# Chunk 0's first channel product as seven block products, its sums on GpSimd

## The chip, the cores and the metric

The kernel runs on one core of a Trainium2 chip. The metric is the device time of one execution in microseconds (us). In the rows below the engines are PE (TensorE, matrix products), PEld (its loading of weights), DVE (VectorE), ACT (ScalarE), POOL (GpSimd) and SP (SyncE, which here only issues transfers). Each engine runs its own instructions strictly in program order and waits on semaphores for the others.

## The reference

Three layers follow one another on 2 batches of 768 tokens, 512 wide:

```
x = attention(q, k, v)          # window of 16 keys to either side, and 24 block summaries
u = x + (relu(x^T @ w_tok1) @ w_tok2)^T            # mixes tokens
y = u + relu(u @ w_ch1) @ w_ch2                    # channel product, width 1536 inside
k = relu((mu_k*y + (1-mu_k)*y_prev) @ w_k)         # second expert layer
r = sigmoid((mu_r*y + (1-mu_r)*y_prev) @ w_r)
out = r * ((k*k) @ w_v)
```

The change concerns `u @ w_ch1`, for the first third of the tokens.

## The kernel before, in words

The 1536 tokens (both batches in a row) are cut into three chunks of 512, numbered 0 to 2. Chunk 0 lies in batch 0 alone, and is ready while the attention of batch 1 still runs, so its channel product shares the engines with that attention. The inner width of 1536 is cut into three blocks d of 512.

Every float32 operand of a large product is held as a high and a low part in a rounded format, and a product takes three matmuls, high by high, high by low and low by high (`mm3`, lines 190 to 192). The high part of a tensor is made on ACT, the low part on DVE by a subtraction. Weights come from memory in packed form, and `ca`, `cn` (ACT) and `cj` (DVE, line 410) unpack them, before `ch` (ACT) and `cl` (DVE, line 417) split them.

The first channel product is computed in two ways:

- Chunk 0: directly. `ch1` (PLAN op `c1`) makes one of 12 tiles of 128 by 512 by 4 by 3 matmuls of 512 columns, from `uc` (u, kept split) and the split weights `wc`. `c1h` and `c1l` (line 469) apply relu and split the result.
- Chunks 1 and 2: by a scheme in which a product of 2 by 2 blocks takes seven block products instead of eight (`product`, op `p`). For each d, each of the seven takes 4 by 3 matmuls of 256 columns. `x_sum` (`bs`, line 643) makes four sums and differences of blocks of u, `x_high` and `x_low` (`bh`, `bl`, line 656) split the seven forms of u. The seven forms of the weights need `form_sum` (`ws e`, line 443), `form_high` (`wh e`) and `form_low` (`wl e`, line 451). `prod_copy` (`pc`, ACT) and seven `prod_add` (`pa`, line 708, DVE) put the seven results together in `ev`, and `h2_high`, `h2_low` (`gh`, `gl`, line 582) apply relu and split.

In the kernel before, the weights of the block products ("e") of d = 0 and 1 are loaded and unpacked a second time (`rawe`); three of the seven forms of d = 1 and 2 are the split weights that chunk 0 uses (`HELD`). Forms are stored to DRAM (`wst`) and loaded again (`wld`) for chunk 2.

The order of all work is written out by hand in the string `PLAN`: the order of its ops is the order of the instructions on each engine. All transfers go through SP's one queue in that order (`load`, line 195), and gates (ops that begin with `g`, such as `gu` and `gx`) are transfers of one element that hold back this queue until the tile they read is there. POOL copies overlapping pieces of v (`vu`, lines 246 to 249) and sets small edges (`pad`, line 317, and `ye`).

Of the kernel before, what the change touches and what calls it, by code (L numbers as in the profile page):

```python
# [55 lines left out]
gv 10,vu 10,gv 11,vu 11,km 1 0,vs 1 10,t2 0 2 0,ca c 0 0,t2l 0 1 0,km 1 3,cj c 0 0,ld c 1 0,t2 0 3 0,ch c 0 0,ca c 1 0
cj c 1 0,gu 0 1 0,t2h 0 2 0,t2l 0 2 0,ch c 1 0,vs 1 11,vs 1 12,sc 6,t2h 0 3 0,cl c 0 0,sc 8,vd 1,t2l 0 3 0,t2 0 0 1,lq 1 2
pad 6,cl c 1 0,t2 0 1 1,max 6,en 6,pad 7,t2h 0 0 1,sc 7,t2h 0 1 1,ef 6,max 7,tr 6 0,pad 8,sc 9,tr 6 1,tc 6 0,max 8,tc 6 1
en 7,t2 0 2 1,pad 9,t2h 0 2 1,ef 7,sc 10,max 9,tr 7 0,en 8,tc 7 0,tr 7 1,pv 6,pad 10,max 10,tc 7 1,ef 8,en 9,ef 9,tr 8 0
norm 6,tr 8 1,sc 11,tc 8 0,tc 8 1,en 10,tr 9 0,pad 11,max 11,ef 10,tr 9 1,pv 7,tc 9 0,tc 9 1,xh 6,t2 0 3 1,en 11,xl 6,ef 11  # L60
norm 7,c1 0 0,t2h 0 3 1,xh 7,xl 7,tr 10 0,c1h 0 0,pv 8,tc 10 0,c1l 0 0,tr 10 1,c1 0 1,norm 8,xh 8,xl 8,tc 10 1,tr 11 0
c1h 0 1,pv 9,tc 11 0,c1l 0 1,tr 11 1,pv 10,norm 9,tc 11 1,xh 9,pv 11,t1 6,xl 9,t1 7,norm 10,xh 10,norm 11,gq 1 0,gq 1 2
ld c 0 1,ca c 0 1,xl 10,gq 1 1,ld c 2 0,ld c 3 0,gu 0 3 1,ld c 1 1,ld c 2 1,ld c 3 1,ca c 3 0,gx 10,ld c 5 1,t1 8,gx 8
ld c 4 0,ld c 5 0,cn c 0 1,ld c 7 0,ca c 2 0,cj c 0 1,cn c 2 0,ld c 4 1,gx 9,ld c 6 0,ld c 6 1,ch c 0 1,cl c 0 1,ld c 11 0
t1 9,cn c 3 0,ld c 8 0,cj c 2 0,ca c 1 1,cj c 3 0,c2 0 0 0,ch c 2 0,c2 0 0 1,ld c 10 0,ch c 3 0,cl c 2 0,cn c 1 1,c2 0 0 2
cl c 3 0,ca c 2 1,ld c 9 0,c2 0 0 3,cj c 1 1,cn c 2 1,c1 0 2,ch c 1 1,cj c 2 1,cl c 1 1,ch c 2 1,ld c 8 1,ca c 5 0,cl c 2 1
t1 10,ca c 4 0,cn c 4 0,c1h 0 2,cj c 4 0,cn c 5 0,c2 0 1 0,c1l 0 2,c2 0 1 1,cj c 5 0,ca c 3 1,ch c 4 0,cl c 4 0,c2 0 1 2
# [101 lines left out]
def block_kernel(ctx: ExitStack, tc: tile.TileContext, qT, kT, vp, w1, w2, wc, wk, wv, wr, mu, mask, const, out):  # L169
# [386 lines left out]
    def ch1_low(c, f):  # L556
        relu_low(h2[c, f], h2p.pop((c, f)))
# [348 lines left out]
```

## Time and profile before

| | |
|---|---|
| median of 3 runs | 457.58 us (457.46 to 459.58) |
| the profiled execution | 462.69 us, of which the span from first to last instruction is 460.9 us |
| mean granted TensorE clock in it | 0.995 |
| PE, DVE, ACT, POOL busy | 447.9, 362.7, 278.4, 39.9 us |

The profiled execution has 1.8 us outside of its span. Busy times are read with care: instructions of one engine overlap somewhat, so the distance between two starts in a row, and not the duration of one, is what an instruction costs an engine that is full.

### The profile page before, as it was taken

How to read it: one execution, taken by the hardware profiler on the slowest of the kernel's cores; microseconds unless marked ns; L12 is line 12 of the kernel's file. 1: busy time of each engine (PE TensorE's matmuls, PEld its weight loads, DVE VectorE, ACT ScalarE, POOL GpSimd, SP SyncE). 2: the span in 40 equal slices, each digit the busy share in tenths (PEclk: the TensorE clock that was granted, in tenths of full speed). 3: DMA queues.
4: the chain of work that ended last, by engine and by line, in shares of the span. 5: the costliest groups of instructions: out<-in, count | busy, mean ns of one | idle time of the engine just before them, and what ended most of it. 6: DMA issues, size and time to landing. Idle time of an engine off the chain costs nothing.

```text
span 460.9 us, 10730 instructions
## 1 busy us (share of the span) xinstructions
PE 447.9 (97%) x4316; PEld 392.0 (85%) x4316; DVE 362.7 (79%) x576; ACT 278.4 (60%) x504; POOL 39.9 (9%) x110
## 2 busy tenths in 40 slices
PE   8799999999999999999999999999999999999996
PEld 3567877888888878989898988888989999999995
DVE  3558978477678637989968819998899989999865
ACT  1377447489987443386635437996887773854530
POOL 1660880000000000000000000000000000000000
PEclk9989999999999999999999999999999999999999
DMA  7767641659745500680597795792979994984902
GB/s 253 233 198 239 202 134 46 233 171 399 300 155 173 219 0 1 221 327 2 173 401 295 279 392 240 297 392 112 352 255 372 369 402 141 348 301 155 337 7 91
DMA packets 33347, 106.23 MB, mean 230 GB/s; under 512 B 3730, under 2 KB 7314, under 8 KB 33298
## 3 DMA queue, kind: packets, MB, share of 16 engines
q1 hardware_dynamic: 33298, 105.55, 62.5%
q8 instruction: 34, 0.56, 0.5%
q14 instruction: 15, 0.12, 0.1%
HBM read 78.79 MB, written 26.74 MB: 229 GB/s over the span
## 4 chain that ended last, share of the span: by engine, by line
PE 83%; DMA 7%; POOL 4%; SPq 3%; DVE 1%; issue 1%; ACT 0%; DVEq 0%; POOLq 0%
PE p L190 9%; PE p L191 9%; PE p L192 9%; PE acc L191 7%; PE acc L192 7%; PE acc L190 7%; PE v L192 4%; PE v L191 4%; PE v L190 4%; DMA rawt<-in_w 3%; SPq L195 3%; PE r L190 2%; PE r L192 2%; PE h L191 2%; PE r L191 2%; PE h L192 2%
## 5 line engine op out<-in xcount | busy, mean ns | idle before, releaser
L708 DVE TENSOR_TENSOR ev<-p,ev 128x512 f32<-128x512 f32 x84 | 56.5, 688 | 19.5 <-PE p L192 16.9
L190 PE MATMUL p<-xs,wba 128*128 128x256 f32 x168 | 47.4, 282 | 0.0
L192 PE MATMUL v<-wbv,k 128*128 128x256 f32 x168 | 47.1, 281 | 0.0
L192 PE MATMUL p<-xs,wba 128*128 128x256 f32 x168 | 47.1, 281 | 0.0
L191 PE MATMUL p<-xs,wba 128*128 128x256 f32 x168 | 47.1, 280 | 0.0
L190 PE MATMUL v<-wbv,k 128*128 128x256 f32 x168 | 47.1, 280 | 0.0
L191 PE MATMUL v<-wbv,k 128*128 128x256 f32 x168 | 47.1, 280 | 0.0
L190 PE MATMUL acc<-hq,wc 128*128 128x512 f32 x96 | 37.8, 393 | 0.0
L191 PE MATMUL acc<-hq,wc 128*128 128x512 f32 x96 | 37.8, 393 | 0.0
L192 PE MATMUL acc<-hq,wc 128*128 128x512 f32 x96 | 37.7, 393 | 0.0
L578 ACT ACTIVATE hq<-ev 128x512 fp32r<-128x512 f32 x24 | 14.9, 631 | 34.3 <-DVE ev L708 31.6
L190 PEld LDWEIGHTS p<-xs,wba 128*128 128x128 f32 x168 | 31.7, 189 | 0.3
L191 PEld LDWEIGHTS p<-xs,wba 128*128 128x128 f32 x168 | 31.7, 189 | 0.1
L190 PEld LDWEIGHTS v<-wbv,k 128*128 128x128 f32 x168 | 31.7, 189 | 0.0
L192 PEld LDWEIGHTS v<-wbv,k 128*128 128x128 f32 x168 | 31.7, 189 | 0.0
L191 PEld LDWEIGHTS v<-wbv,k 128*128 128x128 f32 x168 | 31.7, 189 | 0.0
L192 PEld LDWEIGHTS p<-xs,wba 128*128 128x128 f32 x168 | 31.7, 189 | 0.0
L190 PE MATMUL p<-xs,wae 128*128 128x256 f32 x88 | 24.9, 283 | 0.9 <-DVE ev L708 0.9
L191 PE MATMUL p<-xs,wae 128*128 128x256 f32 x88 | 24.8, 282 | 0.0
L192 PE MATMUL p<-xs,wae 128*128 128x256 f32 x88 | 24.7, 280 | 0.0
L701 ACT COPY ev<-p 128x512 f32<-128x512 f32 x12 | 7.1, 590 | 26.4 <-PE p L192 26.4
L712 ACT ACTIVATE ev<-ev 128x512 f32<-128x512 f32 x24 | 15.0, 631 | 12.4 <-DVE ev L708 12.2
(171 smaller groups left out, 1316.8 us busy)
## 6 DMA issues: line engine op xcount, KB each, us to landing
wba<-kepta SPq DMA_DIRECT2D x28, 512.0 KB
wbv<-keptv SPq DMA_DIRECT2D x28, 512.0 KB
rawc<-in_wc SPq DMA_DIRECT2D x24, 512.0 KB
kepta<-waa SPq DMA_DIRECT2D x14, 512.0 KB
wbe<-kepte SPq DMA_DIRECT2D x14, 512.0 KB
keptv<-wav SPq DMA_DIRECT2D x14, 512.0 KB
rawe<-in_wc SPq DMA_DIRECT2D x8, 512.0 KB
kepte<-wae SPq DMA_DIRECT2D x8, 512.0 KB
```

Source lines behind the costliest of these rows:

```text
L190: PE.matmul(o, lhsT=wh, rhs=xh, start=start, stop=False)
L191: PE.matmul(o, lhsT=wh, rhs=xl, start=False, stop=False)
L192: PE.matmul(o, lhsT=wl, rhs=xh, start=False, stop=stop)
L195: nc.sync.dma_start(out=out, in_=in_)
L578: A.activation(out=h2_block(c, d, q, 0), in_=x, func=AF.Relu)
L701: A.copy(out=block(z, c, d, 0), in_=pr[z, c, d, 0])
L708: V.tensor_tensor(out=block(z, c, d, o), in0=pr[z, c, d, p], in1=block(z, c, d, x), op=ALU.add)
L712: A.activation(out=x, in_=x, func=AF.Relu)
```

## The change

Chunk 0's first channel product is computed by the seven block products too. `ch1` and the split copy `uc` are gone: u of chunk 0 is written unsplit into `y`, as in the other chunks. The block differences of all chunks (`bs` of the channel product) and the weight sums (`ws e`) move from DVE to POOL. All seven forms of the weights of every d are made before chunk 0 needs them, from the one raw load, stored to DRAM, and loaded again for chunks 1 and 2 (`WHICH`). The op counts in `PLAN` change like this: `c1`, `c1h`, `c1l` 12 to 0 each; `p` of the channel product 42 to 63; `pa` 84 to 105 in all; `pc` 12 to 15; `gh`, `gl` 24 to 36; `bh`, `bl` 14 to 21; `bs` 8 to 12; `wh e`, `wl e` 15 to 21; `ws e` 12 as before; `t2l`, `yl` 4 to 0; `ld e` with its `ca`, `cn`, `cj` 8 to 0; `ch c`, `cl c` 24 to 12; `cn c` 22 to 20; `wst e` 14 to 21; `wld e` 14 to 28. The whole string `PLAN` is written anew; chunk 0's and d = 1's block products stand where `c1` stood, and the products of the other chunks take the order d = 2, 1, 0 for chunk 1 and 0, 1, 2 for chunk 2, as before. The number of instructions goes from 563 to 549 on DVE, from 2571 to 2680 on PE, from 110 to 135 on POOL (as the compiled program lists them).

```diff
-norm 7,c1 0 0,t2h 0 3 1,xh 7,xl 7,tr 10 0,c1h 0 0,pv 8,tc 10 0,c1l 0 0,tr 10 1,c1 0 1,norm 8,xh 8,xl 8,tc 10 1,tr 11 0
...
-    HELD = {0: 0, 1: 1, 3: 3}
-
     def form_raw(z, d, j, w):
-        key = ("c", 4 * d + j, 0) if z == "e" and d == 2 else (z, d, j)
-        return words(cv[key], F32)[w]
...
+        return words(cv[("c", 4 * d + j, 0) if z == "e" else (z, d, j)], F32)[w]
...
-        V.tensor_tensor(out=form_raw(z, d, dst, 1), in0=form_raw(z, d, *x), in1=form_raw(z, d, *y),
+        (G if z == "e" else V).tensor_tensor(out=form_raw(z, d, dst, 1), in0=form_raw(z, d, *x), in1=form_raw(z, d, *y),
                         op=ALU.add if z != "v" and j == 0 else ALU.subtract)
...
-    def form_load(z, d, p, n=None):
-        key = (z, d, p) if n is None else (z, d, p, n)
+    def form_load(z, d, p, n):
+        key = (z, d, p, n)
...
+        if (c, dt // 2) not in ys:
+            ys[c, dt // 2] = slot([P, 2, CH + 1], f"y{c}_{dt // 2}")
+        return yk(c, dt)[:, 1 + off:1 + off + n], ps
...
-        A.copy(out=dst if W2[b][g][0] else dst[:, 0], in_=ps)
-
-    def tok2_low(*a):
-        dst, ps = upart(*a)
-        V.tensor_tensor(out=dst[:, 1], in0=ps, in1=dst[:, 0], op=ALU.subtract)
...
+        A.copy(out=dst, in_=ps)
...
-        h = (h2[c, f][:, 0, :], h2[c, f][:, 1, :]) if c == 0 else [hq[c, f // 4, f % 4 // 2, i][:, f % 2, :] for i in range(2)]
+        h = [hq[c, f // 4, f % 4 // 2, i][:, f % 2, :] for i in range(2)]
...
-        V.tensor_tensor(out=xsum(z, c, j), in0=x, in1=y, op=ALU.subtract)
+        (V if z else G).tensor_tensor(out=xsum(z, c, j), in0=x, in1=y, op=ALU.subtract)
...
+    WHICH = {(0, 0): (), (0, 1): (), (0, 2): (), (1, 2): (), (1, 1): (1,), (1, 0): (1,), (2, 0): (1,), (2, 1): (2,), (2, 2): (2,)}
+
     def product(z, c, d, p):
-        if z:
+        if z or c == 0:
             pr[z, c, d, p] = psum(f"p{z}{c}_{d}_{p}")
...
-        w, x = wa["a", d, p, TURN[c, d]] if z else form("e", d, p), xs[z, c, p]
+        w, x = wa["a", d, p, TURN[c, d]] if z else wa[("e", d, p) + WHICH[c, d]], xs[z, c, p]
```

On POOL, around the scores of batch 1, the program before has only the last edges of the attention tiles `e` and then nothing until the edges of `y`, whose tiles are the result of the channel product:

```order
L317 MEMSET e_1392 128x8x8
L317 MEMSET e_1459 128x8x8
L596 MEMSET y_0_2426 128x2
L596 MEMSET y_1_2428 128x2
L598 COPY y_1_1302<-y_1_2428 128x2
L598 COPY y_0_1195<-y_0_2426 128x2
```

After the change the block differences (`xt`, from the blocks of `y`) and the weight sums (in place in `rawc`) stand there, one edge of an attention tile (`e_1408`, query tile 9) behind the first of them, and an instruction named ISA ahead of all:

```order
L320 MEMSET e_1251 128x8x8
L320 MEMSET e_1320 128x8x8
L565 MEMSET y_0_1006 128x2
L608 ISA
L608 TENSOR_TENSOR xt_0_1406<-y_0_1006 128x512
L320 MEMSET e_1408 128x8x8
L437 TENSOR_TENSOR rawc_0_1018<-rawc_0_1018,rawc_0_1067 128x512
L565 MEMSET y_1_1086 128x2
L608 TENSOR_TENSOR xt_0_1406<-y_1_1086,xt_0_1406 128x512
L437 TENSOR_TENSOR rawc_0_994<-rawc_0_1018,rawc_0_994 128x512
L608 TENSOR_TENSOR xt_1_1543<-y_1_1086,y_0_1006 128x512
L608 TENSOR_TENSOR xt_1_1543<-y_1_1086,xt_0_1406 128x512
```

Four sums for d = 1 and four for d = 2 follow directly, then the eight differences of chunks 1 and 2. So POOL gets 24 subtractions and additions, and the tile 9 edge moved behind one of them.

On DVE, at the place of chunk 0's third and fourth direct tiles, the program before unpacks and splits weights (`rawc`, `wc`) and splits the relu of a direct tile (`h`):

```order
L417 TENSOR_TENSOR wc_0_1911<-rawc_0_1797,wc_0_1911 128x512
L410 SCALAR_TENSOR_TENSOR rawc_1_1782<-rawc_1_1782 128x512
L377 TENSOR_TENSOR xhl_1934<-xf_2_1757,xhl_1934 128x512
L417 TENSOR_TENSOR wc_1_1939<-rawc_1_1782,wc_1_1939 128x512
L410 SCALAR_TENSOR_TENSOR rawc_1_1805<-rawc_1_1805 128x512
L469 SCALAR_TENSOR_TENSOR h_0_3_1948<-h_0_3_1915,h_0_3_1948 128x512
L417 TENSOR_TENSOR wc_1_1956<-rawc_1_1805,wc_1_1956 128x512
```

After it, the additions of the block products (`ev`), the low parts of the forms of the weights of d = 1 (`wae`), the unpacking and the splits of the sums (`hq`) stand there without a break:

```order
L412 SCALAR_TENSOR_TENSOR rawc_1_1845<-rawc_1_1845 128x512
L445 TENSOR_TENSOR wae_0_1969<-rawc_0_1814,wae_0_1969 128x512
L552 SCALAR_TENSOR_TENSOR hq_011_1999<-ev_0_1_1723,hq_010_1973 128x2x256
L675 TENSOR_TENSOR ev_0_0_1560<-p_0_3_1945,ev_0_0_1560 128x512
L552 SCALAR_TENSOR_TENSOR hq_001_1820<-ev_0_0_1560,hq_000_1812 128x2x256
L445 TENSOR_TENSOR wae_1_1979<-rawc_0_1818,wae_1_1979 128x512
L552 SCALAR_TENSOR_TENSOR hq_011_1999<-ev_0_0_1560,hq_010_1973 128x2x256
L445 TENSOR_TENSOR wae_5_2032<-rawc_0_1814,wae_5_2032 128x512
L445 TENSOR_TENSOR wae_6_2038<-rawc_0_1848,wae_6_2038 128x512
L445 TENSOR_TENSOR wae_3_1982<-rawc_0_1848,wae_3_1982 128x512
L675 TENSOR_TENSOR ev_1_1_2050<-p_1_1_2013,ev_1_0_2029 128x512
```

Most of these have both inputs in SBUF (the `ev` rows and the `h` row read one from PSUM). So the making of the forms and the putting together of the products moved from a place behind chunk 0 into it.

## Rows read from the trace of the kernel before

**Rows 1.** The page, part 1 and part 2 (busy tenths in 40 slices)

```profile
PE 447.9 (97%) x4316; PEld 392.0 (85%) x4316; DVE 362.7 (79%) x576; ACT 278.4 (60%) x504; POOL 39.9 (9%) x110
POOL 1660880000000000000000000000000000000000
```

**Rows 2.** Waits of PE: line, awaited engine and tile: total us, times, longest

```profile
PE p L190 <- DVE ev L708: 0.9, 1, 0.9
...
PE u L499 <- DVE uc L538: 0.7, 2, 0.5
```

**Rows 3.** Windows: start:end length, busy us of each engine, clock, DMA share, GB/s

```profile
80.00:100.00 20.00, 20.00 (x421) 16.20 (x418) 11.26 (x21) 11.55 (x23) 0.00 (x0) 1.00 0.56 187
100.00:120.00 20.00, 20.00 (x88) 16.21 (x87) 14.39 (x23) 18.52 (x34) 0.00 (x0) 1.00 1.00 383
120.00:140.00 20.00, 20.00 (x96) 16.47 (x96) 15.74 (x26) 17.64 (x33) 0.00 (x0) 1.00 0.48 179
...
180.00:200.00 20.00, 19.12 (x148) 18.26 (x147) 18.82 (x32) 9.85 (x18) 0.59 (x1) 1.00 0.57 205
```

**Rows 4.** Timeline of PE: a direct tile's first matmul, and what follows its twelve

```profile
81.83 0.39 PE L190 MATMUL h<-uc,wc 128*128 128x512 f32 x1
...
84.62 0.60 PE L339 MATMUL et<-cst,e 128*128 128x128 f32 x4
```

**Rows 5.** Timeline of PE: 24 matmuls of block products (first, and next after them)

```profile
175.86 0.28 PE L190 MATMUL p<-xs,wc 128*128 128x256 f32 x1
...
178.65 0.28 PE L190 MATMUL p<-xs,wae 128*128 128x256 f32 x1
```

**Rows 6.** Groups of DVE instructions: busy us, mean ns, idle before them

```profile
L708 DVE TENSOR_TENSOR ev<-p,ev 128x512 f32<-128x512 f32 x84 | 56.5, 688 | 19.5 <-PE p L192 16.9
...
L443 DVE TENSOR_TENSOR rawe<-rawe,rawe 128x512 f32<-128x512 f32 x8 | 5.3, 688 | 0.1
```

**Rows 7.** Timeline of DVE, two instructions back to back

```profile
121.07 0.68 DVE L410 SCALAR_TENSOR_TENSOR rawc<-rawc 128x512 uint32<-128x512 uint32 x1
121.67 0.68 DVE L417 TENSOR_TENSOR wc<-rawc,wc 128x512 fp32r<-128x512 f32 x1
```

**Rows 8.** Timeline of DVE, 46 to 53 us

```profile
47.20 0.88 DVE L377 TENSOR_TENSOR xhl<-xf,xhl 128x512 fp32r<-128x512 f32 x1
48.00 1.69 DVE L410 SCALAR_TENSOR_TENSOR rawt<-rawt 128x512 uint32<-128x512 uint32 x2
49.62 1.09 DVE L417 TENSOR_TENSOR wt<-rawt,wt 128x512 fp32r<-128x512 f32 x1
50.98 0.69 DVE L469 SCALAR_TENSOR_TENSOR h<-t,h 128x512 fp32r<-128x512 f32 x1 [0.26 <-ACT h L466]
51.58 0.94 DVE L417 TENSOR_TENSOR wt<-rawt,wt 128x512 fp32r<-128x512 f32 x1
```

**Rows 9.** Timeline of POOL, 46 to 53 us

```profile
46.73 0.80 POOL L246 COPY vw<-vw 32x520 f32<-32x520 f32 x1 [15.15 <-DMA vw<-in_vp]
...
49.19 0.99 POOL L246 COPY vw<-vw 32x520 f32<-32x520 f32 x1
...
51.36 0.61 POOL L246 COPY vw<-vw 32x520 f32<-32x520 f32 x1
```

**Rows 10.** Timeline of POOL, its last before 164 us

```profile
67.18 0.57 POOL L317 MEMSET e<- 128x64 f32 x6
```

**Rows 11.** Timeline of PE: transposes of tile 9, then a product with v, then u

```profile
78.61 0.87 PE L339 MATMUL et<-cst,e 128*128 128x128 f32 x6
79.41 0.72 PE L350 MATMUL xo<-vbd,et 64*128 64x130 f32 x8
...
80.85 0.44 PE L499 MATMUL u<-cst,xf 128*128 128x128 f32 x2
```

**Rows 12.** DMA issues: the second loads of weights, KB each

```profile
rawe<-in_wc SPq DMA_DIRECT2D x8, 512.0 KB
```

More of the change, by code (lines that the diff above doesn't have):

```diff
@@ new lines @@
+bs 1 1 0,bs 1 1 1,bh 1 1 1,pa 1 0 1 6,v 0 0 6,fs 0 1 3,rst 2 0,bh 1 1 5,bs 1 1 2,fr 0 1 1,bl 1 1 1,vc 0 0,wld v 1 5 0
+fs 0 1 2,ks 0 1 0,fs 0 1 1,bh 1 1 4,bh 1 1 6,bl 1 1 5,v 0 0 1,bh 1 1 2,bl 1 1 6,v 0 0 2,ks 0 1 1,fh 0 1 4,wld v 1 6 0
+bl 1 1 2,fh 0 1 5,fl 0 1 5,v 0 0 3,bs 1 1 3,wld v 1 4 0,bh 1 1 3,ks 0 1 2,p 1 1 1 0,wld v 1 0 0,bl 1 1 4,fh 0 1 1,bl 1 1 3
+wld v 1 1 0,fh 0 1 6,fl 0 1 4,p 1 1 1 1,pc 1 1 1,fl 0 1 6,fh 0 1 3,wld v 1 2 0,ks 0 1 3,p 1 1 1 5,pa 1 1 1 0,fr 1 1 0
+fh 0 1 2,wld v 1 3 0,fl 0 1 1,fs 1 1 0,pa 1 1 1 1,p 1 1 1 6,pa 1 1 1 2,wld a 0 0 1,fh 1 1 0,fl 0 1 3,p 1 1 1 4,mp 2 0 0
@@ L382, in block_kernel @@
                "c": lambda f, i: wc[f][:, 512 * i:512 * i + 512], "r": lambda i: wr[i], "v": lambda d, j: wv[:, d, j],
[L383 to L384 removed]
+               "a": lambda d, j: wk[:, d, j]}
     def fetch(*key):
@@ L420, in block_kernel @@
     wa, kept = {}, {}
-    HELD = {0: 0, 1: 1, 3: 3}
     def form_raw(z, d, j, w):
-        key = ("c", 4 * d + j, 0) if z == "e" and d == 2 else (z, d, j)
-        return words(cv[key], F32)[w]
-    def form(z, d, p):
-        if (z, d, p) not in wa and z == "e" and d and p in HELD:
-            return wt["c", 4 * d + HELD[p], 0]
-        return wa[z, d, p]
+        return words(cv[("c", 4 * d + j, 0) if z == "e" else (z, d, j)], F32)[w]
     FORMS = {"A": (((0, 0), (1, 0), (1, 1), (3, 0), (2, 1), (0, 1), (3, 1)),
@@ L454, in form_store @@
         kept[z, d, p] = d_p.tile([P, 2, 512], F32, tag=f"{z}{d}{p}", name=f"kept{z}{d}_{p}")
-        load(kept[z, d, p], form(z, d, p).bitcast(F32))
-    def form_load(z, d, p, n=None):
-        key = (z, d, p) if n is None else (z, d, p, n)
+        load(kept[z, d, p], wa[z, d, p].bitcast(F32))
+    def form_load(z, d, p, n):
+        key = (z, d, p, n)
         wa[key] = slot([P, 2, 512], f"wb{z}{d}_{p}", F32R)
         load(wa[key].bitcast(F32), kept[z, d, p])
-    h1, uc, t1, ups = {}, {}, {}, {}
+    h1, t1, ups = {}, {}, {}
     def relu_high(dst, ps):
@@ L519, in upart @@
         ps = ups[b, dt, g][:, 0:n]
-        if c:
-            if (c, dt // 2) not in ys:
-                ys[c, dt // 2] = slot([P, 2, CH + 1], f"y{c}_{dt // 2}")
-            return yk(c, dt)[:, 1 + off:1 + off + n], ps
-        if (c, dt) not in uc:
-            uc[c, dt] = slot([P, 2, CH], f"uc{c}_{dt}", F32R)
-        return uc[c, dt][:, :, off:off + n], ps
+        if (c, dt // 2) not in ys:
+            ys[c, dt // 2] = slot([P, 2, CH + 1], f"y{c}_{dt // 2}")
+        return yk(c, dt)[:, 1 + off:1 + off + n], ps
     def tok2_gate(b, dt, g):
-        dst = upart(b, dt, g)[0]
-        gate(dst[:, 0:1] if W2[b][g][0] else dst[:, 1, 0:1].bitcast(F32))
+        gate(upart(b, dt, g)[0][:, 0:1])
     def tok2_high(b, dt, g):
         dst, ps = upart(b, dt, g)
-        A.copy(out=dst if W2[b][g][0] else dst[:, 0], in_=ps)
-    def tok2_low(*a):
-        dst, ps = upart(*a)
-        V.tensor_tensor(out=dst[:, 1], in0=ps, in1=dst[:, 0], op=ALU.subtract)
-    h2, h2p, acc, ys = {}, {}, {}, {}
-    NF = DC // P
-    def ch1(c, f):
-        ps = psum(f"h2_{c}_{f}")
-        h2p[c, f] = ps
-        for k in range(4):
-            u, w = uc[c, k], wt["c", f - f % 4 + f % 4 // 2 * 2 + k // 2, 0]
-            cs = slice(256 * (f % 2) + P * (k % 2), 256 * (f % 2) + P * (k % 2) + P)
-            mm3(ps, w[:, 0, cs], w[:, 1, cs], u[:, 0, :], u[:, 1, :], k == 0, k == 3)
-    def ch1_high(c, f):
-        h2[c, f] = slot([P, 2, CH], f"h2_{c}_{f}", F32R)
-        relu_high(h2[c, f], h2p[c, f])
-    def ch1_low(c, f):
-        relu_low(h2[c, f], h2p.pop((c, f)))
+        A.copy(out=dst, in_=ps)
+    acc, ys = {}, {}
+    NF = DC // P
     def quad(d, c, dt, name, alone=False):
@@ L600, in y_high @@
     def y_high(c, k):
-        V.tensor_tensor(out=yk(c, k)[:, 1:CH + 1], in0=acc[c, k // 2][:, k % 2, :], in1=yk(c, k)[:, 1:CH + 1] if c else uc[c, k][:, 0], op=ALU.add)
-    def y_low(c, k):
-        d = yk(c, k)[:, 1:CH + 1]
-        V.tensor_tensor(out=d, in0=d, in1=uc[c, k][:, 1], op=ALU.add)
+        V.tensor_tensor(out=yk(c, k)[:, 1:CH + 1], in0=acc[c, k // 2][:, k % 2, :], in1=yk(c, k)[:, 1:CH + 1], op=ALU.add)
     xm, mxt, rs, rp, k2 = {}, {}, {}, {}, {}
```

244 lines of the change are left out of this document (120 added, 124 removed).

## The prediction

> **What bounds the kernel now.** I read the page first. PE is busy for 447.9 of the span's 460.9 us, DVE for 362.7, ACT for 278.4, and POOL does nothing after its first sixth [rows 1]. A kernel like this can gain only where PE has less to do or waits less. The list of PE's waits is the second view: it is short, and the two that bear on the edit are u waiting for the split copy `uc` (0.7 us in two places) and one block product waiting 0.9 us for an addition on DVE [rows 2]. So there is little waiting to win, and each wait that the change adds is paid for in full. The third view is the windows around chunk 0's channel product: from 80 to 140 us PE is full, while DVE is busy for 11.3, 14.4 and 15.7 of each 20 us and POOL for none [rows 3]. The last row of that group is the stretch in which DVE was fullest, 18.8 of 20 us, and there PE was busy for 19.12 us: it lost 0.88.
>
> The profiled execution took 462.69 us, 5.1 more than the median of 457.58. All terms below are differences, so I make the sum in that execution and then apply it to the median. About 0.5%, 2.3 us, is what a measurement of this kernel can tell from no change.
>
> **What PE saves.** A direct tile takes 12 matmuls of 512 columns from 81.83 to 84.62 us, 0.2325 us each [rows 4]; 12 tiles are 144 matmuls, 33.5 us. Twenty-four matmuls of 256 columns in block products take from 175.86 to 178.65, 0.116 us each [rows 5]; three times seven products of 12 are 252 matmuls, 29.3 us. PE saves **4.2 us**. The waits for `uc` have nothing to wait for any more, since the low part of u is not made: **0.7 us**. The 0.9 us wait for an addition I leave in, since that kind of wait stays. Together 4.9 us, the most that can come.
>
> **What DVE gets.** In all it has 14 instructions fewer, but that is no measure: before, chunk 0 needed from DVE one relu split per direct tile, and now each block product needs an addition (a product lies in one of two PSUM buffers, so the product after the next waits for it), besides the forms of weights and of u and the splits of the sums. I count the instructions that stand, after the change, between the softmax of the last query tile and the addition of the 14th block product (d = 0 and 1): 62 on DVE, 5 of them short reciprocals. Back to back a full-sized one costs 0.60 us [rows 7], for 0.69 us of duration in its group [rows 6]; 57 are 34.2 us, and with the reciprocals some 35.4. PE's work in the same stretch is 14 products of 12 by 0.116, 19.5 us, and the rest of the attention and of the token mixing: tile 9's transposes, a product with v and a part of u, 3.2 us from 78.61 to 81.83 [rows 4, 11]; two more tiles' transposes, 2 by 0.80; four products with v of 1.44 (79.41 to 80.85) [rows 11], 5.8; six token products of 6 matmuls of 512 columns, 8.4. That is 38.5 us. So DVE is 92% full over 38.5 us, with 3.1 us of slack, where before it was 56 to 79% full. The nearest row is the fullest stretch of before, where PE lost 0.88 in 20 us [rows 3]: over 38.5 us that is **1.8 us** lost. Bounds: 0, if the order suits, and twice that, since there it was one wait that did it.
>
> **What POOL gets.** It gets 24 subtractions and additions of 128 by 512, none of which the trace shows on POOL. The bounds of one are from its copies: 0.61 us for one input of 520 columns alone [rows 9], and twice that, 1.2, for two inputs. I take 1.0, nearer the upper end. The eight for d = 0 need 5 to 10 us; POOL is free from 67.8 [rows 10], and the first product that needs one stands behind two others and most of the attention's end, some 13 us after 81.8 us. So their length as such is hidden by the attention. For d = 1, four of them (2.4 to 4.9 us) stand between rows of DVE that come 4 or more rows ahead of their users; hidden too, if POOL starts when its input is there.
>
> What is not hidden is that they slow DVE. From 46 to 53 us POOL copied next to DVE: DVE's instructions with two inputs in SBUF took 0.88, 1.69 for two, 1.09 and 0.94 us, where 0.69 (1.29 for two) is normal, and the one with an input in PSUM took 0.69 as ever; the POOL copies took up to 0.99 where 0.61 is their own time [rows 8, 9]. DVE lost 0.19, 0.40, 0.40 and 0.25, 1.24 us over six copies, or 0.21 for each. The Trainium skill's page "SBUF — State Buffer", section "Who interferes with whom", says why: a DVE instruction with two SBUF inputs contends with a GpSimd instruction that reads SBUF, and whoever has the shared ports holds the other off completely; the trace agrees in which rows stretch. By that rule taken whole, each subtraction could hold DVE for its full length.
>
> So the price x that one POOL instruction takes from DVE lies between 0.21 us (like a copy) and 1.0 (its whole length). I take **0.5**: it has two inputs where the copy had one, so twice 0.21, and a little more as nearly all DVE rows around it have both inputs in SBUF. Twelve stand in or right ahead of the dense stretch: 12 by 0.5 is 6.0 us, of which DVE's slack takes 3.1, and PE loses **2.9 us**. The four for d = 2 and the eight for chunks 1 and 2 come where DVE is emptier again (its later work shrank by the second unpacking, eight instructions, and by twelve sums): nothing, up to 4 by 0.5. The skill's "GPSIMD Engine Reference", section 3.1, has a POOL add of 2048 columns at 4497 ns, about twice DVE's, by which one of 512 would be an estimated 1.1 us; no run here shows it, and the sum is the same to 0.1 us.
>
> **Other parts at nothing.** ACT loses 14 instructions in all and is 18.5 of 20 us full only from 100 to 120 us [rows 3]; where it is late, DVE is too, and the bound on DVE's lateness holds for both. Transfers: 13 more of 512 KB in all, since the eight second loads go [rows 12] but seven stores and fourteen loads come. At the 383 GB/s of 100 to 120 us one takes 1.4 us. The queue is full in just that window [rows 3], but the loads that stand there (second-half weights, raw weights of d = 2) are used 10 us later and more; the added loads come after 180 us, with a share of 0.57 [rows 3].
>
> **Sum.** 4.2 + 0.7 - 1.8 - 2.9 = 0.2 us faster: 457.4. I say **457.4 us, no change that can be measured**. As a formula: PE loses 12x - 3.1 + 1.8, so the time is 457.58 - 4.9 + 1.8 + (12x - 3.1), the bracket never below zero.
>
> **The rivals.**
>
> 1. The saving arrives. If a POOL instruction costs DVE what a copy did, 12 by 0.21 is 2.5 us, below the slack, and the time is 457.6 - 4.9 + 1.8 = 454.5; if DVE's density costs nothing either, 452.7. For it speaks that nothing else in the rows stands against it; the change is faster by over 0.5% for x below 0.33. Chance 0.33.
> 2. POOL holds DVE for its whole length: x = 1.0, PE loses 10.7 us in the first two blocks of chunk 0, and the time is 463.4. For it speaks that single rows lost 0.40 beside copies of half the length that a subtraction may have [rows 8]; against it, that the mean was 0.21. It is slower by over 0.5% from x = 0.71 on. Chance 0.18.
> 3. The row named ISA ahead of POOL's first subtraction has a price that no row shows, and behind it stands the edge of tile 9's attention weights, for which the exponential and then PE's transposes wait. POOL is free at 67.8 us, a subtraction, the edge and the exponential take some 2, and the transposes, at 78.61 before [rows 10, 11], are asked for some 2 us earlier now: the row has about 7 us for nothing. Each us more delays PE by as much; at 10 us the time is 460.4, slower. Chance 0.06. The skill's "GPSIMD Engine Reference", section 2.1, puts the first call of a freshly loaded kernel at about 6 us more; no run here shows it, and by that figure it is just hidden.
> 4. The queue: the stores of d = 0's and 1's forms stand among the loads in the window that was full. If two stores (2.8 us) come ahead of a load that is needed at once, the time is 460.2. Chance 0.06.
>
> Then 0.37 is left for the forecast. **Range and chances.** The forecast's own range, x from 0.33 to 0.71, is 455.3 to 459.9. To hold 8 in 10 it reaches to the saving with a small loss below (453.0) and into rivals 2 to 4 above (462.0). Faster by over 0.5%: 0.33; within: 0.37; slower: 0.18 + 0.06 + 0.06 = 0.30.
>
> **What would show it.** In the profile of the changed kernel: matmuls of 256 columns at 0.116 us in chunk 0 (the saving); waits of PE on DVE's additions and low parts between 80 and 125 us that sum to about 5 us (forecast), under 2 (rival 1), or 10 (rival 2); POOL's subtractions at about 1.0 us, and DVE's two-input rows beside them at 0.9 to 1.2 us instead of 0.69; the wait of u on `uc` gone; a wait of the transposes on the exponential of tile 9 (rival 3); waits on transfers (rival 4). I am wrong if PE waits little in that stretch though POOL's instructions run beside DVE's, or if the time moves in stretches after 180 us, where I have put nothing.

## The result and the profile after

The changed kernel takes 465.68 us (median of 4 runs, 464.32 to 466.41) against 458.58 for the kernel before on the same chip (457.46 to 459.95): a ratio of 1.0131, with a 95% interval of 1.0101 to 1.0161. It is **slower by 6.0 us** (4.6 to 7.4), and the time lies above the range that was given. The two medians are 7.1 us apart; here and below, differences go by the recorded ratio and not by the medians, which differ from it by up to 0.25%. The profiled execution took 466.09 us, with a span of 464.3. In two runs below, all sums on DVE and the four for d = 1 on DVE, the profiled execution was a slow one, so they give only the time of their other executions.

The first line of the page and two of its strips show what changed as a whole ([rows 1] shows the first two of before; the last line here is the clock's strip of before):

```profile
PE 446.9 (96%) x4424; PEld 395.9 (85%) x4424; DVE 373.0 (80%) x564; ACT 271.8 (59%) x490; POOL 82.5 (18%) x134
...
POOL 1673975305053340000000000000000000000000
PEclk9999999998998999999999999999999999999999
...
PEclk9989999999999999999999999999999999999999
```

POOL has doubled its busy time. DVE has fewer instructions and more busy time, 373.0 us for 564 instead of 362.7 for 576, so some of its instructions have become longer. And TensorE's granted clock has two dips from 100 to 150 us, where before has none; its one dip comes in the third slice, 23 to 35 us.

The windows of the changed kernel over chunk 0's product (busy us of each engine, then clock, DMA share, GB/s), to be held against [rows 3]; the last line is the one of before that [rows 3] lacks:

```profile
80.00:100.00 20.00, 19.53 (x375) 16.43 (x373) 17.83 (x30) 16.52 (x33) 5.74 (x4) 1.00 0.94 317
100.00:120.00 20.00, 15.81 (x105) 14.66 (x105) 18.81 (x24) 13.39 (x24) 7.55 (x4) 0.91 0.75 269
120.00:140.00 20.00, 18.88 (x108) 15.90 (x106) 19.77 (x26) 17.02 (x30) 7.46 (x4) 1.00 0.86 309
140.00:160.00 20.00, 18.77 (x118) 17.10 (x119) 16.02 (x22) 13.98 (x26) 6.23 (x5) 0.91 0.41 158
...
140.00:160.00 20.00, 20.00 (x102) 16.64 (x101) 15.90 (x26) 11.99 (x23) 0.00 (x0) 1.00 0.57 211
```

Before, PE was busy for all of these 80 us. Now it loses 0.47, 4.19, 1.12 and 1.23 us, 7.0 in all. From 100 to 120 us DVE is busy for 18.81 us with 24 instructions, 0.78 us each where 0.60 is the pace of a full DVE.

The waits of PE from 80 to 160 us say for whom:

```profile
PE p L195 <- DVE wae L445: 5.0, 3, 2.7
PE p L193 <- DVE ev L675: 1.5, 2, 1.0
PE xo L360 <- issue: 0.5, 1, 0.5
```

Five of the seven are waits for low parts of forms of weights, `wae`. POOL's timeline has the cause:

```profile
65.96 0.09 POOL L565 MEMSET y<- 128x2 f32 x1
66.14 1.28 POOL L608 TENSOR_TENSOR xt<-y 128x512 f32<-128x512 f32 x1
...
77.45 1.54 POOL L437 TENSOR_TENSOR rawc<-rawc,rawc 128x512 f32<-128x512 f32 x1
...
81.82 3.91 POOL L437 TENSOR_TENSOR rawc<-rawc,rawc 128x512 f32<-128x512 f32 x2
103.85 1.84 POOL L437 TENSOR_TENSOR rawc<-rawc,rawc 128x512 f32<-128x512 f32 x1 [18.12 <-DMA kepte<-wae]
105.78 1.86 POOL L437 TENSOR_TENSOR rawc<-rawc,rawc 128x512 f32<-128x512 f32 x1
107.60 1.97 POOL L437 TENSOR_TENSOR rawc<-rawc,rawc 128x512 f32<-128x512 f32 x1
109.53 1.95 POOL L437 TENSOR_TENSOR rawc<-rawc,rawc 128x512 f32<-128x512 f32 x1
132.46 7.65 POOL L437 TENSOR_TENSOR rawc<-rawc,rawc 128x512 f32<-128x512 f32 x4 [20.98 <-DMA rawc<-in_wc]
```

A block difference takes 1.28 us, a weight sum 1.54, and four weight sums in a row 7.63 (103.85 to 111.48), 1.91 each. The row ISA ahead of the first took no time that can be seen: the memset before it starts at 65.96 and the subtraction at 66.14. DVE beside the four sums that begin at 103.85:

```profile
104.24 2.01 DVE L445 TENSOR_TENSOR wae<-rawc,wae 128x512 fp32r<-128x512 f32 x1
106.17 2.02 DVE L552 SCALAR_TENSOR_TENSOR hq<-ev,hq 128x512 fp32r<-128x512 f32 x1
108.11 0.68 DVE L675 TENSOR_TENSOR ev<-p,ev 128x512 f32<-128x512 f32 x1
108.71 1.41 DVE L552 SCALAR_TENSOR_TENSOR hq<-ev,hq 128x512 fp32r<-128x512 f32 x1
110.05 1.99 DVE L445 TENSOR_TENSOR wae<-rawc,wae 128x512 fp32r<-128x512 f32 x1
111.95 0.68 DVE L552 SCALAR_TENSOR_TENSOR hq<-ev,hq 128x512 fp32r<-128x512 f32 x1
```

Four rows with both inputs in SBUF take 2.01, 2.02, 1.41 and 1.99 us instead of 0.69: 4.67 us more for four sums, **1.17 us for each**. The `ev` row, which reads PSUM, takes its usual 0.68 in the middle of them. The ends of the rows show how: the sums end at 105.69, 107.64, 109.57 and 111.48 us, and the four held rows of DVE at 106.25, 108.19, 110.12 and 112.04, each 0.55 us later. So each held row finishes just behind the sum that it met. DVE has no idle time between these rows; it is the held rows, and not the late arrival of a sum, that make the low parts late. On PE this becomes two waits, and something else behind them:

```profile
112.08 0.38 PE L195 MATMUL p<-xs,wae 128*128 128x256 f32 x1 [2.67 <-DVE wae L445]
112.31 0.28 PE L193 MATMUL p<-xs,wae 128*128 128x256 f32 x1
...
113.69 0.41 PE L195 MATMUL p<-xs,wae 128*128 128x256 f32 x1
113.90 0.41 PE L193 MATMUL p<-xs,wae 128*128 128x256 f32 x1
...
116.68 0.36 PE L194 MATMUL p<-xs,wae 128*128 128x256 f32 x1
```

At first the matmuls follow each other at 0.12 us, then, from 113.7 to 116.7 us, at 0.21: the lower of TensorE's two clock levels, 1.2 instead of 2.4 GHz. Each such spell (the second is behind the waits at 139 to 141 us) costs some 1.5 us, because its 3.4 us hold 16 matmuls that would take 1.9. The sum for this execution is then 7.0 us of waits and 3.1 of lower clock, 10.1, less the 4.9 that PE was to save: 5.2 us slower, and 6.0 (4.6 to 7.4) were measured. The other executions are in line with the price of a spell: two of the four have a mean clock of 0.993 and 0.994 (466.09 and 466.41 us), and two have 0.996, about one spell, and are 1.5 us faster on average (465.27 and 464.32).

### The profile page after: what moved, and what is told of

It is laid out like the page before. It is cut to its first block, busy times and chain, and to the rows that moved or that the text cites. A ratio compares the mean times of both kernels' runs of the same rounds, so it can differ in the third digit from the quotient of the medians.

```text
span 464.3 us, 10957 instructions
## 1 busy us (share of the span) xinstructions
PE 446.9 (96%) x4424; PEld 395.9 (85%) x4424; DVE 373.0 (80%) x564; ACT 271.8 (59%) x490; POOL 82.5 (18%) x134
## 4 chain that ended last, share of the span: by engine, by line
PE 78%; DVE 9%; DMA 6%; ACT 3%; issue 2%; SPq 1%; DVEq 0%; ACTq 0%
PE p L193 9%; PE p L195 9%; PE p L194 9%; PE acc L195 6%; PE acc L193 6%; PE acc L194 6%; PE v L195 4%; PE v L193 4%; PE v L194 4%; PE u L507 3%; DMA vw<-in_vp 3%; PE r L193 2%; PE r L195 2%; PE r L194 2%; DVE rawc L412 2%; DVE wae L445 2%
## 5 line engine op out<-in xcount | busy, mean ns | idle before, releaser
L675 DVE TENSOR_TENSOR ev<-p,ev 128x512 f32<-128x512 f32 x105 | 70.2, 686 | 32.6 <-PE p L195 28.8
L195 PE MATMUL acc<-hq,wc 128*128 128x512 f32 x144 | 56.8, 394 | 0.0
L193 PE MATMUL acc<-hq,wc 128*128 128x512 f32 x144 | 56.7, 394 | 0.0
L194 PE MATMUL acc<-hq,wc 128*128 128x512 f32 x144 | 56.7, 393 | 0.0
L548 ACT ACTIVATE hq<-ev 128x512 fp32r<-128x512 f32 x36 | 22.3, 631 | 44.4 <-DVE ev L675 36.0
L193 PE MATMUL p<-xs,wbe 128*128 128x256 f32 x140 | 39.2, 280 | 0.0
L195 PE MATMUL p<-xs,wbe 128*128 128x256 f32 x140 | 39.1, 280 | 0.0
L194 PE MATMUL p<-xs,wbe 128*128 128x256 f32 x140 | 39.1, 279 | 0.0
L195 PE MATMUL p<-xs,wae 128*128 128x256 f32 x112 | 33.2, 296 | 5.0 <-DVE wae L445 5.0
L193 PE MATMUL p<-xs,wae 128*128 128x256 f32 x112 | 33.5, 299 | 1.6 <-DVE ev L675 1.5
L668 ACT COPY ev<-p 128x512 f32<-128x512 f32 x15 | 8.8, 588 | 42.1 <-PE p L195 41.9
L194 PE MATMUL p<-xs,wae 128*128 128x256 f32 x112 | 32.9, 293 | 0.0
L195 PEld LDWEIGHTS acc<-hq,wc 128*128 128x128 f32 x144 | 27.0, 188 | 6.6 <-DVE wc L419 0.3
L194 PEld LDWEIGHTS acc<-hq,wc 128*128 128x128 f32 x144 | 27.1, 188 | 5.9
L193 PEld LDWEIGHTS acc<-hq,wc 128*128 128x128 f32 x144 | 27.0, 188 | 5.8
L193 PEld LDWEIGHTS p<-xs,wba 128*128 128x128 f32 x168 | 31.7, 189 | 0.2
```

What stands on the lines that cost most here:

```text
L193: PE.matmul(o, lhsT=wh, rhs=xh, start=start, stop=False)
L194: PE.matmul(o, lhsT=wh, rhs=xl, start=False, stop=False)
L195: PE.matmul(o, lhsT=wl, rhs=xh, start=False, stop=stop)
L548: A.activation(out=h2_block(c, d, q, 0), in_=x, func=AF.Relu)
L668: A.copy(out=block(z, c, d, 0), in_=pr[z, c, d, 0])
L675: V.tensor_tensor(out=block(z, c, d, o), in0=pr[z, c, d, p], in1=block(z, c, d, x), op=ALU.add)
```

## The experiments

Theory A: POOL's weight sums hold DVE, PE waits for low parts of forms, and its clock falls behind the waits. Theory B: DVE has too much to do in chunk 0, whatever POOL does. All ratios are to the kernel before, timed on the same chip.

**The eight weight sums of d = 1 and 2 left out, or on DVE.**

```diff
     def form_sum(z, d, j):
+        if z == "e" and d:
+            return
```

> The changed kernel without the eight weight sums for d = 1 and 2 on GpSimd (they are left out, so the forms that need them are made from unsummed weights and the output is not the reference's; every other instruction stays). Theory A (each sum of 1.9 us on GpSimd holds VectorE's two-input instructions for about 1.2 us, TensorE then waits for low parts of forms and falls to its lower clock): VectorE's stretched rows at 104 to 112 and 132 to 140 us are gone, TensorE's waits between 100 and 160 us fall from 6.5 us to under 2, no stretch there shows a granted clock under 0.95, and the time comes down by 7 to 10 us, to 456 to 459. Theory B (VectorE has too many instructions in chunk 0, whatever GpSimd does): waits stay above 4 us and the time above 462.

Measured: 458.43 us, ratio 0.9970 (0.9945 to 0.9995). The windows of that run:

```profile
80.00:100.00 20.00, 19.08 (x372) 16.06 (x369) 18.98 (x32) 14.78 (x28) 4.55 (x3) 1.00 0.94 301
100.00:120.00 20.00, 18.84 (x131) 17.12 (x131) 18.62 (x32) 17.99 (x33) 0.00 (x0) 1.00 0.99 359
120.00:140.00 20.00, 19.91 (x127) 17.48 (x127) 17.18 (x29) 17.70 (x34) 0.27 (x1) 1.00 0.92 333
140.00:160.00 20.00, 19.47 (x109) 16.44 (x109) 17.55 (x19) 11.63 (x21) 11.83 (x8) 1.00 0.23 79
```

PE loses 1.16, 0.09 and 0.53 us from 100 to 160 us, 1.8 instead of 6.5, and the clock stays up. So theory A holds for the loss. But 1.4 us faster is less than the saving of 4.9: over 80 us PE still loses 2.7. Its waits there:

```profile
PE p L193 <- DVE ev L677: 1.5, 2, 1.0
PE xo L353 <- ACT et L346: 0.9, 1, 0.9
PE p L195 <- DVE wae L447: 0.2, 1, 0.2
```

For 1.7 us it waits for DVE, and this is what theory B has right, DVE being busy for 17 to 19 of each 20 us; for 0.9 us it waits for ACT's copy of a tile's transposes.

```diff
-        (G if z == "e" else V).tensor_tensor(out=form_raw(z, d, dst, 1), ...
+        (G if z == "e" and d == 0 else V).tensor_tensor(out=form_raw(z, d, dst, 1), ...
```

> The changed kernel with the eight weight sums for d = 1 and 2 back on VectorE, in the same places of the order; those for d = 0 and the block differences stay on GpSimd. Theory A: VectorE pays 0.60 us for each sum instead of being held 1.2 us, 4.8 us instead of about 9, so TensorE's waits between 100 and 160 us fall from 6.5 us to 2 to 4 and the time to 459 to 462. Theory B: VectorE gets eight instructions more, waits grow to 8 us or more, and the time is 466 or above.

Measured: 460.34 us, ratio 0.9995 (0.9974 to 1.0016), as fast as the kernel before. The same work on DVE is **6 us cheaper** than on POOL. The windows and waits of that run from 80 to 160 us:

```profile
100.00:120.00 20.00, 17.43 (x121) 15.69 (x120) 19.39 (x33) 16.61 (x30) 0.00 (x0) 1.00 0.91 320
120.00:140.00 20.00, 19.90 (x123) 17.36 (x122) 19.39 (x33) 17.68 (x34) 0.00 (x0) 1.00 0.88 332
...
PE p L193 <- ACT wae L442: 2.2, 2, 1.6
```

DVE now does 33 instructions in each 20 us, the most that fit at 0.60 us, and PE waits for the high parts that ACT makes from sums that DVE has made late (ACT stands idle until a sum is there, for 1.23 us shortly before the first of these casts and for 1.37 right before the second).

**All sums and block differences on DVE.**

```diff
-        (G if z == "e" else V).tensor_tensor(out=form_raw(z, d, dst, 1), ...
+        V.tensor_tensor(out=form_raw(z, d, dst, 1), ...
-        (V if z else G).tensor_tensor(out=xsum(z, c, j), in0=x, in1=y, op=ALU.subtract)
+        V.tensor_tensor(out=xsum(z, c, j), in0=x, in1=y, op=ALU.subtract)
```

> The changed kernel with all weight sums and block differences on VectorE, GpSimd as before. Theory A: the first eight (d = 0) held VectorE less, where its rows read PSUM, so this is within 2 us of the run with eight sums on VectorE, to either side, 459 to 463. Theory B: twelve more instructions on VectorE in chunk 0 make it the slowest of all, 467 or above.

Measured: 459.93 us, ratio 0.9992 (0.9969 to 1.0014). The edit moves sixteen instructions more than the run above: the first eight (66 to 86 us) and the differences of chunks 1 and 2. Together they cost and give nothing that can be told within some 1.4 us; the run with only the first eight on POOL, further down, has 0.9995.

**Only the sums and block differences moved, in the kernel before.**

```diff
-        V.tensor_tensor(out=form_raw(z, d, dst, 1), ...
+        (G if z == "e" else V).tensor_tensor(out=form_raw(z, d, dst, 1), ...
-        V.tensor_tensor(out=xsum(z, c, j), in0=x, in1=y, op=ALU.subtract)
+        (V if z else G).tensor_tensor(out=xsum(z, c, j), in0=x, in1=y, op=ALU.subtract)
```

> The kernel before with only its block differences and weight sums moved to GpSimd, in the same places. There VectorE is 50 to 80% full around them. Theory A: GpSimd's instructions take 1.2 to 1.9 us and stretch VectorE rows by up to 1.3 us each, but VectorE has slack, so the time is the same to 3 us slower (458 to 461). Theory B: VectorE is relieved of 20 instructions, same or a little faster (456 to 458).

Measured: 462.51 us, ratio 1.0044 (1.0025 to 1.0064), 2.0 us slower. This is the price without block products in chunk 0, for 20 instructions that DVE no longer has to make, where it is half to nine tenths full. POOL makes four sums from 132.37 to 139.75 us; they and DVE in the timeline:

```profile
132.37 7.38 POOL L443 TENSOR_TENSOR rawc<-rawc,rawc 128x512 f32<-128x512 f32 x4 [67.54 <-PE u L513]
...
130.94 1.29 DVE L410 SCALAR_TENSOR_TENSOR rawc<-rawc 128x512 uint32<-128x512 uint32 x2 [0.31 <-ACT rawc L404]
132.62 3.81 DVE L417 TENSOR_TENSOR wc<-rawc,wc 128x512 fp32r<-128x512 f32 x2 [0.39 <-ACT wc L414]
136.35 3.95 DVE L410 SCALAR_TENSOR_TENSOR rawc<-rawc 128x512 uint32<-128x512 uint32 x2
140.22 0.68 DVE L469 SCALAR_TENSOR_TENSOR h<-h,h 128x512 fp32r<-128x512 f32 x1
```

Pairs that take 1.29 us take 3.81 and 3.95: 5.2 us for four sums, 1.3 each, and here every DVE row beside them has both inputs in SBUF. Again the last held row ends 0.55 us behind the last sum (140.30 and 139.75). Four sums and four held rows: the two engines take turns, one instruction each.

**The dose: four sums twice, and four sums back.**

```diff
+        for _ in range(2 if z == "e" and d == 1 else 1):
+            (G if z == "e" else V).tensor_tensor(out=form_raw(z, d, dst, 1), ...
```

> The changed kernel with each of the four weight sums for d = 1 done twice in a row on GpSimd (the second writes the same values again; everything else stays). Theory A (each such sum holds VectorE, and TensorE waits for it): four more instructions of 1.9 us in the dense stretch, held rows of VectorE for 4 times about 1.2 us and users of the sums later by up to 7.6 us, so TensorE's waits between 100 and 120 us grow from 4.2 to 8 to 11 us and the time by 4 to 8 us over the changed kernel, to a ratio of 1.022 to 1.030. Theory B (VectorE's own number of instructions): no change, ratio 1.013.

Measured: 471.53 us, ratio 1.0247 (1.0225 to 1.0269), 5.3 us more than the changed kernel's 1.0131. Four more sums, 1.3 us of the kernel's time each, waits and clock together. POOL, DVE and the window of that run:

```profile
103.48 15.26 POOL L438 TENSOR_TENSOR rawc<-rawc,rawc 128x512 f32<-128x512 f32 x8 [18.98 <-DVE rawc L412]
...
111.56 1.99 DVE L553 SCALAR_TENSOR_TENSOR hq<-ev,hq 128x512 fp32r<-128x512 f32 x1
113.48 1.98 DVE L446 TENSOR_TENSOR wae<-rawc,wae 128x512 fp32r<-128x512 f32 x1
115.64 3.64 DVE L446 TENSOR_TENSOR wae<-rawc,wae 128x512 fp32r<-128x512 f32 x2 [0.18 <-ACT wae L443]
...
100.00:120.00 20.00, 12.96 (x72) 11.35 (x71) 19.69 (x18) 9.63 (x18) 14.87 (x8) 0.77 0.72 262
```

The held rows go on as long as POOL does, eight of them from 103.86 to 119.28 us, 9.6 us more than 0.69 each: 1.2 us for each sum. DVE completes 18 instructions in 20 us and PE loses 7.0 us in them, a little less than was expected (8 to 11), while the lower clock (0.77 here, 0.88 in the next 20 us) makes up for it. That the time rises by nearly as much for each sum as DVE loses is therefore partly chance.

```diff
-        (G if z == "e" else V).tensor_tensor(out=form_raw(z, d, dst, 1), ...
+        (G if z == "e" and d != 1 else V).tensor_tensor(out=form_raw(z, d, dst, 1), ...
```

> The changed kernel with only the four weight sums for d = 1 on VectorE; those for d = 2 stay on GpSimd at 132 to 140 us. Theory A: the losses of the two groups add up; with both on VectorE the ratio was 0.9995 where the changed kernel had 1.0131, so with one of them about half, 1.004 to 1.009, with TensorE's waits and the lower clock left at 136 to 142 us only. Theory B has the eight as one account of instructions and expects 1.013 or above.

Measured: 462.73 us, ratio 1.0050 (1.0033 to 1.0067), on three executions. The loss splits over the two groups of four, as theory A has it: 3.7 us come back with d = 1, and 2.5 more with d = 2, each known to about 1.5 us.

**Only the first eight on POOL, and DVE's order mended.** The changed kernel with the differences of chunks 1 and 2 on DVE as well:

```diff
+        (G if z == "e" and d == 0 else V).tensor_tensor(out=form_raw(z, d, dst, 1), ...
+        (G if c == 0 and not z else V).tensor_tensor(out=xsum(z, c, j), in0=x, in1=y, op=ALU.subtract)
```

> The changed kernel with only its first eight on GpSimd (block differences and weight sums of chunk 0 and d = 0, at 66 to 86 us); the other sixteen are on VectorE. Theory A: the block differences of chunks 1 and 2 at 140 to 160 us cost a wait of 0.5 us on GpSimd and nothing on VectorE, so within 1 us of the run with eight sums on VectorE, ratio 0.996 to 1.000.

Measured: 459.44 us, ratio 0.9995 (0.9974 to 1.0017), as expected. With this as the base, the order was changed:

```diff
-p 0 0 1 0,gl 0 0 2,pa 0 0 0 6,t1 11,gh 0 0 1,gl 0 0 3,wl e 1 1,wst e 1 1,p 0 0 1 1,ws e 1 0,wh e 1 4,pc 0 0 1,ws e 1 1,wh e 1 5,
-ld c 9 0,ws e 1 2,ca c 2 1,wh e 1 6,gl 0 0 1,wl e 1 5,wst e 1 5,ca c 8 0,wl e 1 6,wl e 1 3,ws e 1 3,wh e 1 2
+p 0 0 1 0,pa 0 0 0 6,t1 11,ws e 1 0,ws e 1 1,wl e 1 1,wst e 1 1,p 0 0 1 1,wh e 1 5,ws e 1 2,ws e 1 3,wh e 1 4,pc 0 0 1,wh e 1 6,
+wh e 1 2,wl e 1 5,wst e 1 5,gh 0 0 1,gl 0 0 2,gl 0 0 3,ld c 9 0,ca c 2 1,gl 0 0 1,ca c 8 0,wl e 1 6,wl e 1 3
```

> The same, and in the order the four sums for d = 1 come together, ahead of three splits of chunk 0's results (low parts of hq) which nothing needs soon, and the second half of their forms' casts right behind them. Theory A: what was left there were waits of 0.6 and 1.6 us on casts of forms that came late from these sums; they shrink to under 0.8 together, the ratio is 0.991 to 0.997. If VectorE has no slack at all there (Theory B), the wait only moves to the next low part or addition, and the ratio stays 0.998 or above.

Measured: 460.13 us, ratio 1.0008 (0.9991 to 1.0025): a miss for theory A, and what B had said. The waits for ACT's casts were gone, and one wait had taken their place, for an addition that the three splits had pushed back, with the clock at 0.91 in its window:

```profile
112.79 0.36 PE L192 MATMUL p<-xs,wae 128*128 128x256 f32 x1 [2.24 <-DVE ev L674]
...
100.00:120.00 20.00, 17.54 (x118) 16.36 (x119) 18.38 (x31) 15.43 (x28) 0.00 (x0) 0.91 0.94 334
```

So the splits were moved again:

```diff
-wl e 1 5,wst e 1 5,gh 0 0 1,gl 0 0 2,gl 0 0 3,ld c 9 0,ca c 2 1,gl 0 0 1,ca c 8 0,wl e 1 6,wl e 1 3,pa 0 0 1 0,gh 0 1 0,t1h 1 0,p 0 0 1 5,pa 0 0 1 1
+wl e 1 5,wst e 1 5,gh 0 0 1,ld c 9 0,ca c 2 1,ca c 8 0,wl e 1 6,wl e 1 3,pa 0 0 1 0,gl 0 0 2,gl 0 0 3,gh 0 1 0,t1h 1 0,p 0 0 1 5,pa 0 0 1 1,gl 0 0 1
```

> The reordered kernel with the three low parts of hq moved once more, from ahead of the addition of d = 1's second block product to behind it and behind the next one (the place where that run showed its last wait, 2.2 us for that addition). If VectorE's order alone makes the wait, the wait falls under 0.7 us, no stretch shows the lower clock, and the ratio is 0.990 to 0.997. If VectorE is simply full from 100 to 116 us, a wait of 1.5 us or more comes back at the next low part or addition and the ratio stays 0.997 to 1.001.

Measured: 459.62 us, ratio 0.9994 (0.9973 to 1.0015). Neither forecast came whole. The waits and the clock are those of the first (under or at 0.7 us, 1.00), the ratio is that of the second. PE's loss from 100 to 120 us fell from 2.46 to 1.56 us, but the time did not follow clear of noise. What waits are left are at the next rows of DVE, which is now busy for 19.90 of 20 us:

```profile
111.62 0.36 PE L192 MATMUL p<-xs,wae 128*128 128x256 f32 x1 [0.56 <-DVE ev L674]
114.53 0.39 PE L194 MATMUL p<-xs,wae 128*128 128x256 f32 x1 [0.70 <-DVE wae L444]
...
100.00:120.00 20.00, 18.44 (x126) 16.20 (x125) 19.90 (x34) 16.64 (x30) 0.00 (x0) 1.00 0.92 335
```

In the run beside it, tile 11's transposes and copy (`tr 11 1`, `tc 11 1`) stood right behind `norm 10` instead of behind `wh e 0 4`.

> The same with the transposes of query tile 11's far part, and their copy on ScalarE, moved ahead of two casts of weights, so that the product with v at 91 us no longer waits 0.9 us for the copy. If that wait is on the path, 0.5 to 1.5 us less than the run beside it (0.2 to 0.3%); if VectorE sets the pace behind it, no difference.

Measured: 459.15 us, ratio 0.9994 (0.9975 to 1.0013). The wait of 0.9 us for the copy was gone, but 0.35 us for an earlier copy and 0.49 for an addition at 100 us came in its place. No difference in time by the ratio (0.5 us by the medians).

**The start of the order.** The string of the order was written anew from its first operation on, and in this last pair of runs the first 158 operations (batch 0's attention) were exchanged between the two kernels.

> The last kernel (sums for d = 1 and 2 on VectorE, splits behind the addition, tile 11 ahead) with the first 158 operations of the order, up to the split of batch 0's fifth tile, put back in the order of the kernel before; all else stays. In the profiles the changed kernels reach the first matmul of u at 50.9 to 51.8 us, the kernel before with its sums on GpSimd at 48.9. If the new order of the start costs this, the time falls by 1 to 2.5 us, to a ratio of 0.994 to 0.998, and u begins at 49 to 50 us. If it is scatter between executions (loads of v in the first 25 us), the ratio stays at 0.998 to 1.001.

Measured: 458.0 us, ratio 0.9964 (0.9938 to 0.9990), the lowest ratio of a complete kernel here, 1.7 us faster than the kernel before. But u began at 54.3 us in its profiled execution, not at 49 to 50, so the reason given was not seen. That execution cannot refute it either: it was the slowest of the twelve (461.47 us), with a wait of 1.93 us at 42.7 us and the lower clock behind it.

> The kernel before with its first 158 operations in the order of the changed kernel. If the new start costs 1 to 2.5 us, the ratio is 1.002 to 1.006 and u begins at 51 to 52 us; if it is scatter, 0.999 to 1.001.

Measured: 460.25 us, ratio 1.0005 (0.9988 to 1.0023): no cost of the new start can be told in the kernel before. In its profiled execution u began at 51.7 us; the kernel before has 51.8 in its own. Together the two leave the share of the start open, between nothing and some 1.5 us.

## Why the prediction was wrong

**PE's saving was right.** Block products ran at 0.12 us per matmul of 256 columns in chunk 0, and the waits for `uc` are gone. No run measures the saving alone; the run without the eight sums fits it: 4.9 less 2.7 us of waits is 2.2, and 1.4 (0.2 to 2.5) was measured.

**DVE's density was about right.** The 1.8 us (between 0 and 3.6; 0.88 in 20 us over 38.5 is in fact 1.7) measured 1.2 in that run from 80 to 120 us, and 1.7 up to 160 us. The other 0.9 us was a wait for ACT, which I had put at nothing. That what is left is DVE's fullness and not the order is argued, not shown: the reorderings moved or shortened the waits (2.57, 2.46, 1.56 us lost from 100 to 120) without a change of the time that can be told from noise.

**The step that failed is the price x** ("So the price x that one POOL instruction takes from DVE lies between 0.21 us (like a copy) and 1.0 (its whole length). I take 0.5"). It measured 1.17 us in the changed kernel, 1.2 where four sums were doubled, and 1.3 in the kernel before with its sums moved, all above the upper end of the bound. One reason is the length: a weight sum takes 1.5 us alone and 1.9 next to DVE, not 1.0. The other is that I carried a mean over from short instructions to long ones, and read [rows 8] and [rows 9] apart. Side by side they have the same ends as the sums: copies end at 47.53, 50.18 and 51.97 us, and held rows of DVE at 48.08, 50.71 and 52.52, each some 0.55 us later. A row was held to the end of the copy that it met, and only so little, 0.19 to 0.40 us, because the copies were short (0.61 us alone for the longest). What a sum takes from DVE is nearly its whole length, less the part in which DVE reads PSUM (the row of 1.41 us). The rule of the Trainium skill's page "SBUF — State Buffer", section "Who interferes with whom", taken whole, was the better guide: it has whoever holds the shared ports keep the other off completely, and the rows above agree. Rival 2 is what happened, in its mechanism; 0.18 was too small a chance.

**"Nothing, up to 4 by 0.5" for d = 2 was wrong too.** I had DVE emptier after the second block. From 120 to 140 us it was busy for 19.8 of 20 us with the sums for d = 2 beside it (17.2 in the run without them), and moving them to DVE brought 2.5 us back.

**The first eight, which I counted in at the full price, cost nothing that can be measured.** They ran at 66 to 86 us, beside rows that read PSUM or behind which there was time. That the formula gives 465.4 with x = 1.17, near the measured 465.68, is therefore luck, errors that cancel: eight instructions counted that cost nothing or little, four left out that cost as much as any, and no term for the clock.

**The clock had no term.** In two spells of 3.4 us PE ran at its lower level behind its waits, 3.1 us in all, half of the net loss. In [rows 3] the clock was at 1.00 in every window, and I never asked what a wait does to it. The trace of before had a case of it outside [rows 3], a wait of 1.99 us and a window clock of 0.91:

```profile
21.52 0.67 PE L272 MATMUL vs<-vw,cst 128*64 128x130 f32 x8 [1.99 <-DMA vw<-in_vp]
...
20.00:40.00 20.00, 17.75 (x481) 13.51 (x482) 11.80 (x20) 13.66 (x30) 10.69 (x29) 0.91 0.69 217
```

**The other rivals did not come.** ISA: 0.18 us from the memset's start to the subtraction's. The Trainium skill's "GPSIMD Engine Reference", section 2.1, has about 6 us for a first call of a freshly loaded kernel; no such time shows in this run. The queue: PE has no wait for a transfer from 80 to 160 us. The price for an add in section 3.1 of the Trainium skill's "GPSIMD Engine Reference", by which a sum would be an estimated 1.1 us, is near the block differences (1.28 alone) and below the weight sums (1.54 alone); why the latter are longer was not tried.

## What to carry to other kernels

An idle GpSimd is no free second VectorE. Before work with SBUF inputs is moved there, count the DVE rows that will run beside it with both inputs in SBUF: here such rows and the sums took turns, so moving 0.6 us of work cost DVE 1.2 to 1.3 us; the moves that cost nothing were those beside rows that read PSUM, or where nobody waited. When a price is taken from rows of another operation, look at where the two engines' rows end, and not only at the mean. And when a change adds waits of PE, look at the granted clock behind them: here a wait cost the wait and nearly half as much again (7.0 and 3.1 us).

## What the runs showed of the hardware

- GpSimd and VectorE take turns by whole instructions where VectorE has both inputs in SBUF: a held row ends some 0.55 us behind the end of the GpSimd instruction that it met, beside copies in the kernel before, and beside sums in the changed kernel and in the kernel before with its sums moved. VectorE's rows went from 0.69 to 2.0 us, and GpSimd's sums from 1.54 to 1.91. A row with an input in PSUM stayed at 0.68.
- TensorE's lower clock came behind single waits of 2.67 us (changed kernel), 2.24 (the reordered run) and 1.99 (kernel before), behind two of 0.96 and 0.82 us close together (changed kernel, 139 to 141 us), and behind 0.37 and 1.18 us (the run with only the first eight on POOL, 92 to 94 us). Windows with waits of 0.62 and 1.55 us apart, or 0.56 and 0.70, stayed at 1.00. So it is not only waits of over 2 us that bring it, and no run here says which do.
